# Half of the score masks and the experts' weights on ScalarE, longer DRAM packets and a new written order in a fused S4 convolution and mixture-of-experts kernel

## The chip, the cores and the metric

The kernel runs on one core of a Trainium2 chip. The metric is device time in microseconds (us). Before the change the median of three runs is 816.15 us (811.91 to 817.66); a fourth execution was taken with the hardware profiler.

The core's engines run side by side, each through its own list of instructions in order: TensorE (PE in the profile; its weight loads are PEld), VectorE (DVE), ScalarE (ACT), GpSimd (POOL) and SyncE (SP). SP issues most DMA transfers, and POOL issues the indirect gathers and the accumulating stores. 16 DMA engines carry all of them.

## The reference, cut to what matters

```python
x = A_u                       # [1, 2048, 448]
xn = _layernorm(x)
return x + _A_ref(xn, ...) + _B_ref(xn, ...)

def _A_ref(u, A_re, A_im, B_re, B_im, C_re, C_im, log_dt, Dskip):
    P = jnp.exp(logdA[:, :, None] * l[None, None, :])     # [448, 256, 2048], complex
    K = jnp.einsum("dn,dnl,dn->dl", Cc, P, dB).real
    ...                       # y = causal convolution of u with K over L = 2048, by FFT
    return y + u * Dskip

def _B_ref(x, w_q, k1, k2, u, v):     # 16 heads, 64 + 64 keys, 4096 experts, K = 1
    q = jnp.einsum("nd,dhc->nhc", xf, w_q)
    s1 = jnp.einsum("nhd,ed->nhe", q[..., :dk], k1)
    s2 = jnp.einsum("nhd,ed->nhe", q[..., dk:], k2)
    ...                       # best key of each half gives the expert, e = i1 * 64 + i2
    act = _gelu(jnp.einsum("nd,nhkd->nhk", xf, u[top_e]))
    out = jnp.einsum("nhk,nhk,nhkd->nd", g, act, v[top_e])
    return out
```

## The kernel before, in words

**Work.** The 2048 tokens are 16 tiles of 128; the 448 channels are four chunks (128, 128, 128, 64).

- *Weights.* `combine` loads the query weights of each of 16 heads (`wq`, L855, two loads of 448 KB a head) and multiplies them by the keys, so a score is one product with a token tile. `params` loads the six S4 parameter arrays (L419) and prepares exponents and phases.
- *Score stage, 16 tiles.* `ln` normalizes a tile. `score` forms 32 rows of 64 scores a token: TensorE writes four quarters `sc` of 128x512 into PSUM (L961, L970). They and other products share the tag `s2`, which has three buffers. VectorE takes each row's maximum (`mx`, L985). A mask of the places that are not the maximum follows: for quarters 0, 1 and 2 VectorE does it in one `not_equal` (L992), for quarter 3 ScalarE does eight `Sign` activations of 128x64 (L996). The option `SG` is the number of quarters that ScalarE takes. A quarter's buffer is free when its mask is done. From the masks VectorE finds the expert numbers, which go through DRAM to become gather indices.
- *S4 kernel, 56 batches of eight channels.* `batch` and `products` build powers of the state matrix: phases on VectorE (L614), sines and absolute values on ScalarE (L629 to L635), exponentials on ScalarE (L590, L592), products on VectorE (L660 to L666), then small matmuls (L682, L702).
- *Convolution.* `conv` does a transform for each chunk. Its result `tq` goes to the DRAM scratch `t_d` (L842), 512 bytes a packet in the three wide chunks.
- *Experts, 16 tiles of four groups.* For each group of four heads four indirect gathers bring 128 rows of 896 floats (`ue`, L1083). VectorE multiplies the first half by the token and sums it (`dot`, L1091). Then, on 128x4 values: a square on ScalarE (L1098), a product on VectorE (L1101), the gate's product on VectorE (L1110), tanh on ScalarE (L1104), a product on VectorE (L1107). VectorE spreads the four weights over a 0/1 mask into `A`, 128x128 (L1114), and TensorE adds the weighted second halves into `po` (L1121). When the four groups are in, ScalarE copies `po` out (L1132), and POOL adds it onto the output in DRAM (L1135).
- *Final.* For each chunk `final` loads `t_d` back (`tl`, L1165), multiplies (L1177), and adds to the output; for the last chunk it loads the output so far (`bb`, L1155), adds on VectorE (L1181) and stores (L1189).

**What sets the order.** Each stage adds steps to a plan: a stream name, an engine, a cost in ns, the instructions, and the buffers that it takes and gives. The order is written out by hand as a string, `ORDER` (L173 to L202): each character names a stream (its place in `CODE`), and each occurrence issues that stream's next step. The string has 3421 steps. Each engine works through its steps in this order, and a step that is not ready holds up what is behind it on its engine. Buffers of the tag `q` (22 of 128x1024) hold gathers, score weights, transform inputs and loads alike; a gather can start when an earlier holder has been released.

Of the kernel before, what the change touches and what calls it, by code (L numbers as in the profile page):

```python
# [32 lines left out]
def shape_consts():  # L33
# [17 lines left out]
    pe = 2 * np.pi * (np.outer(k2, b) % 64) / 64  # L51
# [64 lines left out]
class Plan:  # L116
# [57 lines left out]
    "41H444446H4447H244024HHHH424HH6H4H2H7H12H4HHHHHII7H42H1HNCC42H7282O42D2E842HH8748HH121CDH4CD2KHF4HEE1D14E224HFL4H4CKL7DC"  # L174
    "I472K24F72EC4I4F3MD7777E7Y3C5QFJLKL9D56DCEFEP47F48D47C9F9EM8KQLQ48D9FwK97774E7FC4L8K44DCJA947E449YC87C9JFDD47E46H7RF4798"
    "AL8QRCEARF7ADCZDEDRFEFEFKQRHwQLNORHGQ9RHQQPH9SaRRMRTQZHTRQYQNATRRHTRHHJOATSTQQTTTTBRTeHReTTGQTUVQGHbYVMHHWRRQQHHXHxxcHee"
    "RRRPdfSNgxgOyfeHgHHwgQwQIHHIyxPfQKyHgygzggxRQJ!gRT!gHhRYTQLTGRzHgQhTKh#xgHRLxTfRMRNOPeSQygyJxXgx#TQ$yTxgeHQHTfQTyTThxTzR"
    "!HgRg!bHxTfgxRgzTQRe#Q#yyyUycgdz$NybxxRO!Qch!ezRyVQHhH#Rdebyi#STTVIIgxRRHThhYwj$gwyzh!QxK!wgyHQzWTLHRwRQKxLRQHRxy#TN#kR$"
    "HxPMhShghyxyxHOHizxaygHQXH!TyxTjTeK!QThJLTyy%kbXeRzhHRQ&RQKRiJzxP#jHf!Qg#$!eyHHLYRQzhggHkfRghieHHRxxgxSf#jK#ykTyI$lLKTgg"
    "LMeTyZlzmTKm!x!LlKyxzmLlN#xUHM#Tyx$IOgggTxgQTYQwKPhHHQyHfHQyTRwgzLwg!R!gQxhgRhRKgzMhyHTe#HfJHgHw#gLmQxHeehxx$yRyhiNRReeO"  # L180
    "yxjkfgzQQ!gVHVhSP!xg%yTyHzJxTyTHx#QRT#gHxTTyQglRHzThchQ$gH!hTIMdKgg!YQR&TIxRRLWmyYKLiNJhjhzfyR#OgUJk#R$ihaQHjexPyVyHxHeH"
    "zKSkMxgegy!x!hHQfTLHRKzyTexLgMR#g#eVQhfH$HbRgQgwQwglhyWxwZTxXygghyHwHzlRggRmHmH!Yg!TRzyTxiQf#xjke#RHy$HSNOHHIyhxTxlTz!TT"
    "TXXK!yTghQLTzQ#yeTPegxhKhgJhx%#fgmeyxgyIQxyezyLifg$Hjg!cQbRkRhKTg!YgLRzxlKh#UQHg#MgVgx$dQygaRLxHiNyhHxHmzOfPQeygw!R!xjhy"
    "ggzkefgyRRSgxyQ&##RHwQRThhzRVw!HHH$fxTQl!zH##QRehHQgRgiyRHHxgeWRSxewNMHjHxO$HhkTIyhgQgZKLyTxQhlJyTxmyTgKLRigmTQzhx!T!zIx"
    "#xygyMfJ%xgJXTQyPeRRTRg#hx$TgTjfzekQKgy!TRgx!Lxfyhz#y#lTegQRxKUgc$LmeNRSVxVeayOhWhzywQ!hTQiQyRjxgy!hQzygwhRPhXzgxgMT#Rxk"
# [12 lines left out]
    "ezhgfwyjgwey-gex#yg#xeiyzgxyg!kal$yj!zx%yxhyxghmkz#hc!#hg$ydglxeghfyymggixfgheyegfe!jzh#k#xezg!ylg!Zxgzxhggyy#iggh$yhz#$"
    "wwg!jhkmlymxfwoheyxexh!giphgwqego&oypfxepqqyz#ohx#yxggoz!ppfqg!yjy$gxzeoyr#gqxxozphngigqkoxpgs#%aq!yxo!z$yhpg#ghqejsfpno"
    "gehyrggphs&hyxe#tzfgq$kegofgnxygi!qg!jhexzphxouxqpo#gvnk#ghyqywwpxgwhg$qsihgojyfyezg!kx!pzqopehetgrghhsshoyny#whfuglxlx#"  # L200
    "qmpgymiefvjhgzx$egxgykulx!gmlg!x%yqytxnihymzglgghxhxghr&shhhzixjs#j#k!lvh$mmy!kizxt##jlkyl(ymum$vooqoqyzqy!x!rs)yq,qsqry"
    "(*zsosrsq#xy(zsq)!+!r)*sts+t#t$t*(z#.#+$%.)/:&.-//.::/*;+;;:;")  # L202


class Kernel:
    OPT = dict(UE=8, XX=4, CS=2, ZI=2, MG=4, KT=4, HL=2, SG=1, XR=4, OB=3, XT=1, ST=1)
# [21 lines left out]
    def alloc(s):  # L228
# [11 lines left out]
        s.t_d = dr.tile([64, 2, 32, D], F32, name="t_d")  # L240
# [146 lines left out]
    def params(s, part):  # L387
# [349 lines left out]
    def conv(s, ck, VK):  # L737
        p = s.p
# [31 lines left out]
        for q in range(4):  # L770
# [76 lines left out]
    def combine(s, h):  # L847
# [219 lines left out]
    def experts(s, t):  # L1067
# [9 lines left out]
        for g in range(4):  # L1077
            Q = {}
            u = (4 * t + g) / 64
            for c in range(4):  # L1080
# [25 lines left out]
            def v2(Q=Q):  # L1106
                s.nc.vector.scalar_tensor_tensor(Q["th"], Q["th"], 1.0, Q["dot"], op0=ALU.add, op1=ALU.mult)  # L1107

            def v2b(g=g, Q=Q):
                s.nc.vector.tensor_tensor(out=Q["dot"], in0=Q["dot"], in1=s.IDX[t][:, :, 4 + g].bitcast(F32), op=ALU.mult)  # L1110

            def v2c(Q=Q):
                Q["A"] = s.sm.tile([128, 4, 32], F32, name="A", bufs=2)
                s.nc.vector.tensor_tensor(out=Q["A"], in0=s.mask[:, None, :].to_broadcast([128, 4, 32]),  # L1114
                                          in1=Q["th"][:, :, None].to_broadcast([128, 4, 32]), op=ALU.mult)
# [23 lines left out]
    def final(s, ck):  # L1139
# [20 lines left out]
        for g in range(4):  # L1160
            B = {}

            def l1(B=B, g=g):
                B["tl"] = s.flat("q", "tl", 8 * w).rearrange("p (x d) -> p x d", x=8)
                s.nc.sync.dma_start(B["tl"], s.t_d.rearrange("(x c) r k d -> x (c r k) d", c=2)[8 * g:8 * g + 8, :, d0:d0 + w].rearrange("x p d -> p x d"))  # L1165
# [95 lines left out]
```

## Time and profile before

| | |
|---|---|
| Median of three runs | 816.15 us (811.91 to 817.66) |
| Profiled execution | 807.42 us, its span 805.7 us |
| Mean granted TensorE clock | 0.906 |
| Gathers (L1083) on POOL | 256, 308.2 us |
| Score matmuls (L961) | 384, 181.2 us |
| Experts' dots (L1091) | 256, 155.7 us |
| Changes of ScalarE's table in the exponentials and the sines (L590, L639) | 54 loads of 1.283 us |

The page names an instruction by engine, line, operation and tiles, `out<-in`. A group's row gives its count, busy time in us and mean ns of one behind the bar, and then the engine's idle time just before the group with what ended it. Where instructions of a group overlap, busy time is less than count times mean. A row of a stretch gives from:to, its length, the busy time of each engine (and how many instructions), the granted TensorE clock, the busy share of the 16 DMA engines and GB/s. A wait's row gives us in total, times, and the longest. The chain of waits is the work that ended last, followed back from the end.

### The profile page before, as it was taken

The page shows a single profiled execution, that of the slowest core. Times are in us where ns is not written, and L with a number is a line of the kernel's source. Part 1 is how long each engine was busy: PE and PEld are TensorE (multiplying, and loading weights), DVE is VectorE, ACT ScalarE, POOL GpSimd, SP SyncE. Part 2 cuts the span into 40 slices and gives each one's busy share as a digit, 9 for nine tenths or more (in the row PEclk, how much of TensorE's full clock was granted, in tenths as well). Part 3 has the DMA queues.
Part 4 walks back from the last instruction along what each step waited for, and adds up shares of the span by engine and source line. Part 5 has one row for each costly group of instructions (what it writes and reads, how often), then busy time and mean ns, then how long its engine had stood idle before and what let it go on. Part 6 is the DMA issues. An engine that isn't in the chain of part 4 may idle for free.

```text
span 805.7 us, 19880 instructions
## 1 busy us (share of the span) xinstructions
PE 664.6 (82%) x7628; PEld 361.1 (45%) x7628; DVE 686.9 (85%) x1727; ACT 533.3 (66%) x1069; POOL 351.6 (44%) x303
## 2 busy tenths in 40 slices
PE   1999999989999899799887877778885865899693
PEld 0433333343443334344364644445663532567472
DVE  6885678998899989799998989899998888999850
ACT  1665246538576676564567868888788887888630
POOL 2020033234333435347745474765364557643521
PEclk9999999999999999999999995678997665699896
DMA  9997666778867668588999998999699999889899
GB/s 313 348 335 263 259 224 175 232 204 249 275 199 242 202 202 255 180 252 270 366 300 312 304 286 286 292 291 276 206 286 344 319 222 269 252 264 287 271 253 175
DMA packets 139975, 212.36 MB, mean 264 GB/s; under 512 B 45096, under 2 KB 121896, under 8 KB 139816
## 3 DMA queue, kind: packets, MB, share of 16 engines
q0 software_dynamic: 29120, 124.27, 49.9%
q1 hardware_dynamic: 110760, 86.81, 35.5%
q8 instruction: 60, 0.98, 0.5%
q14 instruction: 35, 0.29, 0.1%
HBM read 181.42 MB, written 33.29 MB: 267 GB/s over the span
## 4 chain that ended last, share of the span: by engine, by line
DVE 33%; PE 24%; ACT 15%; DMA 15%; issue 9%; POOL 2%; SPq 1%; POOLq 0%; DVEq 0%; ACTq 0%
PE sc L961 8%; DVE ue L1091 7%; DMA ue<-in_uv_dram,ig 6%; DVE ph L614 4%; PE wc L862 3%; DVE mg L666 3%; PE po L1121 3%; DVE zi L662 2%; DVE cp L808 2%; ACT CS L635 2%; DVE mx L985 2%; ACT CS L629 2%; ACT CS L632 2%; PE sc L970 2%; PE up L724 2%
## 5 line engine op out<-in xcount | busy, mean ns | idle before, releaser
L1083 POOL DMA_INDIRECT ue<-in_uv_dram,ig x256 | 308.2, 1204 | 364.2 <-PE po L1121 101.4
L961 PE MATMUL sc<-W,xt 128*128 128x512 f32 x384 | 181.2, 611 | 8.6 <-ACT xt L946 7.8
L1091 DVE SCALAR_TENSOR_TENSOR ue<-ue,xr 128x448 f32<-128x448 f32 x256 | 155.7, 619 | 26.0 <-DMA ue<-in_uv_dram,ig 24.1
L961 PEld LDWEIGHTS sc<-W,xt 128*128 128x128 f32 x384 | 69.3, 191 | 100.8 <-issue 86.2
L1121 PE MATMUL po<-ue,A 128*32 128x448 f32 x512 | 74.0, 654 | 23.4 <-DVE A L1114 9.2
L682 PE MATMUL kp<-mg 128*32 128x64 f32 x1792 | 65.8, 244 | 22.2 <-DVE mg L666 7.9
L590 ACT ACTIVATE mg<-lg 128x512 f32<-128x512 f32 x112 | 63.1, 603 | 17.2 <-PE lg L579 16.7
L682 PEld LDWEIGHTS kp<-mg 128*32 128x32 f32 x1792 | 48.1, 124 | 49.4 <-issue 13.2
L662 DVE TENSOR_TENSOR zi<-mg,CS 128x1024 f32<-128x1024 f32 x56 | 68.3, 1219 | 0.0
L666 DVE TENSOR_TENSOR mg<-mg,CS 128x1024 f32<-128x1024 f32 x56 | 68.3, 1219 | 0.0
L682 PE MATMUL kp<-zi 128*32 128x64 f32 x1792 | 65.7, 242 | 0.0
L614 DVE CUSTOM_DVE_ANT_0 ph<-st,ph 128x512 uint16<-128x512 uint16 (+2 forms) x84 | 65.2, 776 | 0.5
L635 ACT ACTIVATE CS<-CS,halfpi 128x1024 f32<-128x1024 f32 x56 | 64.4, 1150 | 0.8
L629 ACT ACTIVATE CS<-ph 128x1024 f32<-128x1024 int32 x56 | 62.0, 1107 | 3.9 <-DVE ph L614 3.1
L632 ACT ACTIVATE CS<-ph 128x1024 f32<-128x1024 int32 x56 | 62.6, 1117 | 0.0
L702 PE MATMUL vp<-f,kt 128*64 128x128 f32 x448 | 41.3, 317 | 19.5 <-DVE kt L693 11.3
L985 DVE TENSOR_REDUCE mx<-sc 128x8 f32<-128x512 f32 x64 | 43.7, 683 | 14.5 <-PE sc L970 9.6
L682 PEld LDWEIGHTS kp<-zi 128*32 128x32 f32 x1792 | 50.3, 126 | 0.2
L579 PE MATMUL lg<-lc,rt 32*128 32x512 f32 x112 | 38.8, 544 | 12.0 <-ACT mg L590 7.9
L830 PE MATMUL ip<-cp,e 64*128 64x256 f32 x384 | 44.7, 382 | 2.9 <-DVE cp L808 2.8
L702 PEld LDWEIGHTS vp<-f,kt 128*64 128x64 f32 x448 | 27.5, 155 | 43.1 <-DVE kt L693 16.7
L798 PE MATMUL U<-VU,g 128*64 128x128 f32 x384 | 41.3, 294 | 6.0 <-ACT us L803 3.4
(244 smaller groups left out, 1219.2 us busy)
## 6 DMA issues: line engine op xcount, KB each, us to landing
wq<-in_wq_dram SPq DMA_DIRECT2D x32, 448.0 KB
xr<-xn_d SPq DMA_DIRECT2D x64, 224.0 KB
vu_d<-vst SPq DMA_DIRECT2D x64, 112.0 KB
VU<-vu_d SPq DMA_DIRECT2D x12, 512.0 KB
t_d<-tq SPq DMA_DIRECT2D x24, 256.0 KB
tl<-t_d SPq DMA_DIRECT2D x12, 512.0 KB
ue<-in_uv_dram,ig POOLq DMA_INDIRECT x256
xx<-in_x_dram SPq DMA_DIRECT2D x16, 224.0 KB
```

Of the source, the lines that this page charges most:

```text
L614: s.nc.vector.tensor_tensor(out=rw(n, 2 * n), in0=rw(0, n), in1=o["st"][:, k, b0:b0 + 2].rearrange("p b h m x -> p (b h m x)")[:, None].to ...
L629: s.nc.scalar.activation(CS[:, 1].rearrange("p (m r x) -> p m r x", r=16, x=2), four(s.ph), AF.Sin, scale=SC)
L632: s.nc.scalar.activation(B["CS"][:, 0].rearrange("p (m r x) -> p m r x", r=16, x=2), four(s.ph), AF.Abs)
L635: s.nc.scalar.activation(B["CS"][:, 0], B["CS"][:, 0], AF.Sin, scale=-SC, bias=s.halfpi)
L662: V.tensor_tensor(out=zi[:, 512:], in0=mg[:, 512:], in1=CS[:, 1], op=ALU.mult)
L666: V.tensor_tensor(out=mg[:, 512:], in0=mg[:, 512:], in1=CS[:, 0], op=ALU.mult)
L682: s.nc.tensor.matmul(kp[32 * c:32 * c + 32, 64 * gi:64 * gi + 64], T[ri][:, 1024 + m:1056 + m], view(T[ri], m, [[512, 2], [1, 32]]), start ...
L702: s.nc.tensor.matmul(vp[64 * ri:64 * ri + 64, 128 * gi:128 * gi + 128], B["kt"][:, 64 * gi:64 * gi + 64], s.f1[:, ri], start=True, stop=True)
L961: s.nc.tensor.matmul(B["sc", q].rearrange("p a b -> p (a b)"), B["xt"][:, i], w, start=(q % 2 == 0 and i == 0), stop=(q % 2 == 1 and i == 2))
L1083: s.nc.gpsimd.indirect_dma_start(out=ue, out_offset=None, in_=s.io["uv"], in_offset=bass.IndirectOffsetOnAxis(ap=s.IDX[t][:, c, g:g + 1].b ...
L1091: s.nc.vector.scalar_tensor_tensor(Q["ue", c][:, :D], Q["ue", c][:, :D], 1.0, B["xr", c], op0=ALU.mult, op1=ALU.mult, accum_out=Q["dot"][: ...
L1121: s.nc.tensor.matmul(B["po"][32 * c:32 * c + 32, :D], Q["A"][:, c], Q["ue", c][:, D:], start=(g == 0), stop=(g == 3))
```

## The change

- `SG` goes from 1 to 2: quarter 2's mask is also made by eight `Sign` activations on ScalarE.
- The four experts' weights of a group are spread by four ScalarE copies of 128x32, each with a per-partition scale (a new stream `e_A`), in place of VectorE's one product of 128x128.
- The product of the dots with the gate is written to a tile of its own, `dw`, instead of over `dot`. It depends on the dots alone, and the tanh no longer waits for it.
- Layouts in DRAM: `wq` and the six parameter arrays are stored so that one partition's row is one run of 3584 bytes instead of two of 1792. `t_d` becomes one array a chunk, with the two parities of the block number apart; the transform's constant `e` is permuted to match. The store keeps packets of one channel row (512 bytes in the wide chunks). The load reads eight such rows in one run (4096 bytes), with two transfers of 64 partitions in place of one of 128.
- A new `ORDER`, again of 3421 steps. Near the end all four loads of the last chunk stand ahead of the last load of the output so far.

```diff
-    pe = 2 * np.pi * (np.outer(k2, b) % 64) / 64
+    pe = 2 * np.pi * (np.outer(k2, b.reshape(32, 2).T.reshape(64)) % 64) / 64
...
 ORDER = (
-    "41H444446H4447H244024HHHH424HH6H4H2H7H12H4HHHHHII7H42H1HNCC42H7282O42D2E842HH8748HH121CDH4CD2KHF4HEE1D14E224HFL4H4CKL7DC"
...
+    "444441442H4142444424HH7HH2H1HH227HHHH444HHH2HHHH26IN2HH444I4H6CH74H701CHD4HD18E2HH4HC28E8DO4H47CFCK28DD72HH2ILFEC44EECFK"
...
-    OPT = dict(UE=8, XX=4, CS=2, ZI=2, MG=4, KT=4, HL=2, SG=1, XR=4, OB=3, XT=1, ST=1)
+    OPT = dict(UE=8, XX=4, CS=2, ZI=2, MG=4, KT=4, HL=2, SG=2, XR=4, OB=3, XT=1, ST=1)
...
-        s.t_d = dr.tile([64, 2, 32, D], F32, name="t_d")
+        s.t_d = [dr.tile([2, 32, 2, 32, w], F32, name="t_d%d" % i) for i, (d0, w) in enumerate(s.chunks)]
...
-                s.nc.sync.dma_start(B[n], io[n].rearrange("(t p) d -> p t d", p=128))
+                s.nc.sync.dma_start(B[n], io[n])
...
-                    s.nc.sync.dma_start(s.t_d[:, ri, 8 * q:8 * q + 8, d0:d0 + w],
+                    s.nc.sync.dma_start(s.t_d[ck][ri, 8 * q:8 * q + 8].rearrange("k c x d -> (c x) k d"),
                                         Q["tq"][64 * ri:64 * ri + 64].rearrange("p k h d -> p (k h) d"))
...
-                s.nc.sync.dma_start(B["w", sd], s.io["wq"][h, sd].rearrange("t p d -> p t d"))
+                s.nc.sync.dma_start(B["w", sd], s.io["wq"][h, sd])
...
-                        for k in ("dot", "x2", "th"):
+                        for k in ("dot", "x2", "th", "dw"):
...
             def v2(Q=Q):
-                s.nc.vector.scalar_tensor_tensor(Q["th"], Q["th"], 1.0, Q["dot"], op0=ALU.add, op1=ALU.mult)
+                s.nc.vector.scalar_tensor_tensor(Q["th"], Q["th"], 1.0, Q["dw"], op0=ALU.add, op1=ALU.mult)
 
             def v2b(g=g, Q=Q):
-                s.nc.vector.tensor_tensor(out=Q["dot"], in0=Q["dot"], in1=s.IDX[t][:, :, 4 + g].bitcast(F32), op=ALU.mult)
+                s.nc.vector.tensor_tensor(out=Q["dw"], in0=Q["dot"], in1=s.IDX[t][:, :, 4 + g].bitcast(F32), op=ALU.mult)
 
             def v2c(Q=Q):
                 Q["A"] = s.sm.tile([128, 4, 32], F32, name="A", bufs=2)
-                s.nc.vector.tensor_tensor(out=Q["A"], in0=s.mask[:, None, :].to_broadcast([128, 4, 32]),
-                                          in1=Q["th"][:, :, None].to_broadcast([128, 4, 32]), op=ALU.mult)
+                for c in range(4):
+                    s.nc.scalar.activation(Q["A"][:, c], s.mask, AF.Copy, scale=Q["th"][:, c:c + 1])
...
-            y = p.chain("e_v1", "DVE", [(75, v1), (75, v2b)], deps=[y])
+            y = p.add("e_v1", "DVE", 75, v1, deps=[y])
+            yw = p.add("e_v1", "DVE", 75, v2b, deps=[v])
             y = p.add("e_a", "ACT", 100, a2, deps=[y], tset="E|S|A")
-            y = p.chain("e_v2", "DVE", [(75, v2), (dv(128), v2c)], deps=[y, s.C["mask"]], take=("A",), give=("gel",))
+            y = p.add("e_v2", "DVE", 75, v2, deps=[y, yw])
+            y = p.add("e_A", "ACT", 460, v2c, deps=[y, s.C["mask"]], take=("A",), give=("gel",))
...
-                s.nc.sync.dma_start(B["tl"], s.t_d.rearrange("(x c) r k d -> x (c r k) d", c=2)[8 * g:8 * g + 8, :, d0:d0 + w].rearrange("x p d -> p x d"))
+                for c in range(2):
+                    s.nc.sync.dma_start(B["tl"][64 * c:64 * c + 64], s.t_d[ck].rearrange("r k c x d -> c (r k) x d")[c, :, 8 * g:8 * g + 8])
...
-        wq=np.ascontiguousarray(f("B_w_q").reshape(D, 16, 2, 2, 128).transpose(1, 2, 3, 4, 0)),
+        wq=np.ascontiguousarray(f("B_w_q").reshape(D, 16, 2, 2, 128).transpose(1, 2, 4, 3, 0)),
...
-        **{n: tr("A_" + n) for n in ("A_re", "A_im", "B_re", "B_im", "C_re", "C_im")},
+        **{n: np.ascontiguousarray(tr("A_" + n).reshape(2, 128, D).transpose(1, 0, 2)) for n in ("A_re", "A_im", "B_re", "B_im", "C_re", "C_im")},
```

More of the change, by code (lines that the diff above doesn't have):

```diff
@@ L178 @@
[L178 to L185, printed above, removed]
@@ new lines @@
+    "#HHHTTxxyIy$QR%gRQfTxeNTxhhyyxhThyzIO!yg!ISizzJ!!z#Mhjg$#TRwhYZU$HSKJYwHQTeQgHTR%HLQHRKQ%LggcHRwHJVxdQxwygycHHQxNHRxOihT"
+    "yhQHTTxHhRHVRHHahgSyMQSKzLkT!z&gPQihTKy!HjgIxxTx#yTTj$TRdykQIyzfWR%LRgRhQxThRQgfKS!khPiLzgXxljY!HeRMTe#$gmxSlkfxxKyyy%Lg"
+    "Y(yKHgmLMTKLzxlH!JUNeO!Gz#Hgx$QmeyexgHyhggQ%gKLyRQhbgfhHyQhRxQgxwMzxwgRRHgHHHT!!ze#Pfxhgg$QlfKRTyee%RVHwLygHyHTN&hwOyHSz"
+    "QHT!HxmITeh!hzSe#QiRQxjg$kVRxgIMgZXyxTyyyhz!zYg!gPa#Tc%x$lhKQJRTQyL%xxYgdgmHHxHeRhygyiTKQRTHRjTThLTNWxOxfSSkeHQgijHygKTe"
@@ new lines @@
+    "hyyJTUzLMVeQfKhg(xQgVL!f!ezxRyH#QyghgM$hwbXgxz%ixPgR!kbQlzR!XgwwgThHRJHRYQlgmWxTgejR#khySHx$%yfNHSywThgHyHHeHOzQgHh!TIKL"
+    "xexxzmK!g&QLyIeT#hlfxgZygHimyMyz$T!Y%Rzxf!xK#TgThRTgHjhkTegQx$LHhHcKQdRHTghTPgTyUgiQ%gjHHyXxQLgNfRhayHyRgheezHOS!HgPzxQg"
+    "lRm!HhHV#fQyQHSggxHxyykxHxyfz!hHR$wIMTRVRRwQ%QgQgNTTRghlhe!TRzOx#yexxyeiQSITwyS$wK%JQyjzggghTkhilRh!QRmgxjxTzgPTTh!mT&#L"
+    "KfQg$gTLgxexxT%JfQyeeRZb(xTKQyyyzgLKTUgRye!!zyR#fexLyM$gxyhRahNzO%xgghywxQikySgQQ!lwJVgxzScxy!yjR#$%RVRkxgzQhh!gziQQxdNj"
@@ new lines @@
+    "yhTwTgTTRleRxSm!TJXwmR#ekyxO$xxhShZyhP%&xyyxQfggbzMgyTyP!Wxe!QxRQTlTeTfzyQTR#Tgg$zfTRx%QgiTy!yxyQxxjhRyT!eRzzgn!h#h!$%yR"
+    "yhkUnnXNgOzgQilVhSx#yxS$%ymgz!QgmjgQ!QThfRwgWzgwnwxwygTxRkhygf#$ReVe%xQgRxgfeeyPlyxzgQmgg&hx!coexx!aRhyyRzSySyxzh!Tp!#Tx"
+    "gxzT$xyqx%nhxox#oyyiT(pyxz$!TxyTTq!hyTXz%wgdjpky#nbxo(xqxnwpoyghigpgzqe$gfgqohgWrpfT!wgTgheo!hfhqTssxogeepzoxyqTig%pUVqt"
+    "#epgXyhjwy.$hgrgZnx%yhokjg&sqhggypyikoezx!yqyhoz!xx(xfgpge#$zVyyqg!%fyxspoe!qhegzgxfgop#pgxxyhqoh$qpzjxyek!hcoglygztygrx"
@@ new lines @@
+    "!yhd#z!Xmw%qhglpm$xisjlmsqibjwzgyhk!krfx#gwaxwxglhWg%xh$gmlmslf%yggfgetheyiehehgygmexyh&zhgjsgixhkh!y!yxlgxmfyxxxgzjgzh!"
+    "gzekl!hm#$h%ihgehyg#x(xxyyy$fxxyzgg!ehejtf!gieyyggzZgkhyh#lg%g)*jzmghg+hZigck$wajxhd!ykfw%gle!eze)gh#$fhxgegwyh%fg&wyygg"
+    "egz!xzhi*h+jglxgmx)ky!#m$gxxflxyy%h,xh)ygzhmyh!e!egggyij(xxzefx#gykeey$ynwhgywxh*f+%gggz!!gglgzx(ia#hhgmj*hkgelyweywbXh+"
+    "gehzXm$fgigfjggfgxy,xghe!xchh%x,ek!zglgxgdxg#mi$xhh%y,hjgkyxlmxonyhygzgifepgyoxgxhoq!hfyzpq&oyjp!qoe#pz!!z$obx#$gxnqyepg"
```

32 lines of the change are left out of this document (12 added, 20 removed).

## The prediction

> **What bounds the kernel now.** I read the page's first line, engine shares and chain first, then the DMA queues, then the stretches, because the kernel has stages with different limits. I cut it at 60 us (weights loaded), 405 us (last score tile's signs done) and 750 us (tail).
>
> ```profile
> span 805.7 us, 19880 instructions
> PE 664.6 (82%) x7628; PEld 361.1 (45%) x7628; DVE 686.9 (85%) x1727; ACT 533.3 (66%) x1069; POOL 351.6 (44%) x303
> DVE 33%; PE 24%; ACT 15%; DMA 15%; issue 9%; POOL 2%; SPq 1%; POOLq 0%; DVEq 0%; ACTq 0%
> q0 software_dynamic: 29120, 124.27, 49.9%
> q1 hardware_dynamic: 110760, 86.81, 35.5%
> ```
>
> No engine is full: VectorE, TensorE and the DMA engines each work over 80% of the span, and the chain changes hands.
>
> ```profile
> core 0: us, PE busy (x) PEld busy (x) DVE busy (x) ACT busy (x) POOL busy (x), PEclk, DMA share, GB/s
> 0.00:60.00 60.00, 40.85 (x167) 16.92 (x169) 47.12 (x79) 29.93 (x65) 9.42 (x19) 1.00 0.97 331
> 60.00:405.00 345.00, 317.63 (x2195) 135.12 (x2193) 301.42 (x802) 202.38 (x455) 133.09 (x117) 0.99 0.76 239
> 405.00:750.00 345.00, 269.22 (x4504) 181.09 (x4500) 315.09 (x786) 283.66 (x511) 193.75 (x155) 0.82 0.93 281
> 750.00:806.00 56.00, 36.91 (x768) 27.95 (x768) 23.29 (x63) 17.28 (x40) 15.30 (x15) 0.80 0.94 230
> ```
>
> Three things to see. The first 60 us are loads (DMA share 0.97). From 60 to 405 us TensorE is fullest: 317.6 of 345 us (92%), idle 27.4, with VectorE at 301.4 (87%) and ScalarE at only 202.4 (59%). From 405 to 750 us VectorE leads with 315.1 of 345 (91.3%), and ScalarE is no longer a spare engine: 283.7 (82%).
>
> **The change part by part.**
>
> ```profile
> L992 DVE TENSOR_TENSOR eq<-sc,mx 128x512 bf16<-128x512 f32 x48 | 32.9, 686 | 2.9 <-DMA vu_d<-vst 2.6
> L996 ACT ACTIVATE eq<-sc,mx 128x64 bf16<-128x64 f32 x128 | 27.9, 333 | 14.5 <-DVE mx L985 14.4
> L996 ACT ACTIVATE eq<-sc,mx x128: 306/332/376, 81.0 to 403.3; 128x64 bf16<-128x64 f32 x128
> L1114 DVE TENSOR_TENSOR A<-mask,th 128x128 f32<-128x128 f32 x64 | 18.3, 286 | 0.5
> L1110 DVE TENSOR_TENSOR dot<-dot,ig 128x4 f32<-128x4 f32 x64 | 10.2, 160 | 0.4
> ```
>
> *Masks.* Each of 16 tiles has four score quarters; one more goes from VectorE to ScalarE. VectorE loses 16 x 0.686 = 11.0 us. ScalarE gains 16 blocks of eight signs, 27.9/16 = 1.74 us each: 27.9 us. The signs run from 81.0 to 403.3 us (smallest, median and largest are 306, 332 and 376 ns), so all of this lies before 405 us.
>
> *Experts' weights.* 64 VectorE products of 0.286 us go (18.3 us); 256 ScalarE copies of 128x32 with a per-partition scale come. No row shows that copy. The nearest is the sign of 128x64, which also reads a per-partition operand: one alone takes 333 ns, but eight together 1.74 us, so the next begins (1740-333)/7 = 201 ns after the last. A column costs about 0.83 ns (128x512 against 128x126 out of PSUM, rows below: (603-276)/386 = 0.85). With 32 columns fewer I estimate 306 ns alone, 175 ns between starts, a group of four 3 x 175 + 306 = 0.83 us, 64 of them 53 us. Ends: 0.57 us (four copies 90 ns apart, as the 128x4 square below, which starts at 530.36 and is followed at 530.45, plus one of 306 ns) and 1.22 us (four that don't overlap). I take 0.83, since the sign is the nearest.
>
> ```profile
> L590 ACT ACTIVATE mg<-lg 128x512 f32<-128x512 f32 x112 | 63.1, 603 | 17.2 <-PE lg L579 16.7
> L690 ACT ACTIVATE kt<-kp 128x126 f32<-128x126 f32 x56 | 15.4, 276 | 13.6 <-PE kp L682 13.4
> 530.36 0.21 ACT L1098 ACTIVATE x<-dot 128x4 f32<-128x4 f32 x1
> 530.45 1.10 ACT L632 ACTIVATE CS<-ph 128x1024 f32<-128x1024 int32 x1
> ```
>
> [...]
>
> How they fall on the stages:
>
> ```profile
> 60.00:405.00 345.00, 7.11 (x25) 0.99 0.76 239
> 405.00:750.00 345.00, 10.02 (x35) 0.82 0.93 281
> 750.00:806.00 56.00, 1.16 (x4) 0.80 0.94 230
> ```
>
> (L1114's VectorE time alone.) To 405 us VectorE loses 11.0 + 7.1 = 18.1 us, ScalarE gains 27.9 + 25 x 0.83 = 48.7, to 251 of 345 (73%). From 405 to 750 VectorE falls to 305.1, ScalarE rises by 35 x 0.83 = 29.0 to 312.7 (90.6%): the two change places.
>
> *Dots in a tile of their own.* The L1110 product leaves the path between the two ScalarE steps: 0.16 us a group shorter. The weights' copies make the path 0.83 - 0.29 = 0.54 longer and put a second trip to ScalarE into it, where they queue behind exponentials and sines. Behind them wait the po matmuls, whatever TensorE has after those, and the gathers, whose buffers these matmuls free:
>
> ```profile
> PEld po L1121 <- DVE A L1114: 16.6, 19, 2.0
> POOL ue L1083 <- PE po L1121: 101.4, 31, 8.5
> ```
>
> So +0.38 us a group, 24 us over 64 groups if nothing covered it. The cover is distance in the written order: I counted steps from a group's first gather to its po matmul, median 115 of 3421 before and 106.5 after; last weight to matmul, 10 and 10. The new order makes the round shorter, so I cost the latency at nothing; without that cover it is up to the 24 us.
>
> *Long packets.* wq and the six parameter loads go from 256 to 128 packets each, tl from 1024 to 128: 38 x 128 + 16 x 896 = 19,200 packets fewer of 139,975, same bytes. q1's packets average 784 B and 16 x 0.355 x 805.7/110760 = 41 ns, q0's 4268 B and 221 ns: 53 and 52 ns per KB, so a fixed cost per packet does not show (saving 0). The other end, 41 ns for any packet spared, is 19,200 x 41/16 = 49 us of DMA time, 7 us at DMA's 15% of the chain. I take 2.5: 1 in the loads, 1.5 from 405 us on. tl becomes two transfers, 16 more issues on SP; one took 0.44 us (row below, under the written order), 7 us, spread over SP's waits and 1.8 us in the tail.
>
> [...]
>
> *Written order.* Exp and sine still alternate: 60 changes of table set counted in either order. The four residual copies (input to output, in DRAM) move from steps 275 to 420 to steps 286 to 743, further into the stretch where the DMA share is 0.76; I cost that at nothing, with the idle quarter of the DMA engines as the cover. In the tail SP waits for the last output and only then issues the last tl load:
>
> ```profile
> 787.25 6.86 DMA out_dram<-ob
> 794.12 0.67 SPq L1155
> 794.91 0.44 SPq L1165 DMA_DIRECT2D tl<-t_d  x1
> 794.91 3.88 DMA tl<-t_d
> 798.93 1.11 PE po L1177 x32
> 800.07 0.42 DVE bb L1181
> ```
>
> The new order issues all four tl loads ahead of that wait, so 3.88 us leave; the last base load (issued at 794.12, its first use at the earliest some 2 us later) is late next. I take -2.5, of which the extra issues give 1 back: -1.5.
>
> *Sum.* Loads -1. To 405 us: between 18.1 x 33% (VectorE's share of the chain) = 6.0 and all 18.1; TensorE is fullest and I take -8. From 405 to 750: the fullest engine was 91.3% busy; ScalarE's 312.7 at that share is 342.5 us (-2.5), VectorE's 305.1 would be 334 (-11); I take the later, -2.5, and -1.5 for packets. Tail -1.5. Total -14.5 from this execution's 807.4 (span 805.7 and 1.7 around it): 792.9. The median of the runs shown, 816.15, lies 8.7 above this execution, so 801.6.
>
> **The rivals.**
>
> *VectorE was the only bound (faster still).* All -18.1, -11, -1, -1.5, -1.5: -33.1, 783 on the median's scale. Against it: TensorE has only 27.4 us idle to 405 us, and ScalarE is at 90% later.
>
> *ScalarE takes the place (no change).* If the four copies do not overlap (1.22 us), ScalarE has 283.7 + 35 x 1.22 = 326.4 us, at 91.3% full 357.5: +12.5 where I have -2.5. Total +0.5: 816.6. For it: the rows above at 82% already.
>
> *PSUM banks are held too long (slower).* A score bank is free after its mask, 0.69 us on VectorE, now 1.74 us on ScalarE plus its queue there; three banks serve four quarters of a tile, and TensorE, with 27.4 us of slack, waits in order.
>
> ```profile
> ACT eq L996 <- DVE mx L985: 14.4, 7, 4.0
> ```
>
> That row says the sign mostly waits for nothing but its turn. If the turn comes behind a sine block's half (1.7 us), 16 x (1.05 + 1.7) = 44 us of later release; half of it on TensorE is 22, and the -8 is gone: 807.4 - 1 + 22 - 4 - 1.5 = 822.9, 831.6 on the median's scale. It eats the whole gain from 14.5 us of lost TensorE time on.
>
> *The granted clock falls (slower).* Rows of the same kernel at two clocks:
>
> ```profile
> 600.00:650.00 50.00, 34.66 (x592) 20.30 (x588) 44.02 (x106) 43.71 (x76) 28.34 (x24) 0.76 1.05 317
> 650.00:700.00 50.00, 35.04 (x510) 19.25 (x512) 44.05 (x115) 40.86 (x71) 31.13 (x25) 0.56 0.88 256
> 745.57 0.96 PE L1121 MATMUL po<-ue,A 128*32 128x448 f32 x8
> 762.64 1.72 PE L1121 MATMUL po<-ue,A 128*32 128x448 f32 x8
> ```
>
> If waits for ScalarE bring 405 to 750 us to the 0.66 of these two stretches, TensorE's 269.2 us become 269.2 x 0.82/0.66 = 334, 366 at 91.3% full: +21 for my -2.5. Total +9, 825. [...]
>
> **How the numbers follow.** My sum 0.44; VectorE alone 0.09; ScalarE in its place 0.19; banks 0.15; clock 0.13. A measurement tells about 1% (8 us) from no change. My case holds 790 to 812 around 801.6; a fifth of it, 0.08, is above 808, as its 14.5 us gain is the size of the latency I cost at nothing. Faster: 0.36 + 0.09 = 0.45, and 0.05 of ScalarE's case where VectorE gains more early: 0.50. Same: 0.08 + 0.14 = 0.22. Slower (above 824.3): 0.28. The range goes from 786, leaving out most of VectorE alone (0.07), to 830, leaving out half the slower cases (0.12).
>
> **What would show it.** Right: VectorE near 658 us, ScalarE near 614; the weights' line at 0.83 us a group; TensorE over 92% busy to 405 us; ScalarE fullest after; no tl load behind the last base load. Wrong: copies near 1.2 us a group; TensorE waiting for signs; a clock below 0.75 after 405 us; gathers waiting for po matmuls well over 101 us.

## The result and the profile after

The changed kernel takes 820.65 us (median of 20 runs, 816.17 to 825.20) against 814.65 us of the kernel before beside it (20 runs): a ratio of 1.0127 with a 95% interval of [1.0096, 1.0158]. That ratio is taken over each kernel's runs within 1.5% of its fastest, which leaves out 7 of the 20 runs before, and so is larger than the ratio of the two medians, 1.0074. The change is slower by 6 to 10 us, where the prediction said 1.8% faster. The profiled execution took 818.54 us. Its page begins, in the order of the lines shown of before (span, engines, chain, q1):

```profile
span 815.5 us, 20337 instructions
PE 679.4 (83%) x7628; PEld 376.5 (46%) x7628; DVE 663.4 (81%) x1647; ACT 609.2 (75%) x1453; POOL 344.6 (42%) x303
PE 38%; ACT 22%; DMA 17%; DVE 13%; issue 5%; POOL 1%; SPq 1%; ACTq 0%; DVEq 0%; POOLq 0%
q1 hardware_dynamic: 91816, 86.82, 35.2%
```

The engines were relieved and loaded nearly as planned: VectorE lost 23.5 us (686.9 to 663.4; 29.3 were planned), ScalarE gained 75.9 (533.3 to 609.2; 80.9 were planned). In the chain VectorE fell from 33% to 13%, but TensorE rose from 24% to 38% and ScalarE from 15% to 22%. On q1 19,000 packets are gone, and their time is what it was: 0.352 x 815.5 = 287 us of 16 engines, 0.355 x 805.7 = 286 before.

The stretches, cut as before, show TensorE at 320.9 of 345 us (93%) up to 405 us, VectorE down to 291.2 there, and ScalarE level with VectorE after 405:

```profile
0.00:60.00 60.00, 39.96 (x175) 16.47 (x177) 40.74 (x72) 29.12 (x64) 8.54 (x18) 1.00 0.91 321
60.00:405.00 345.00, 320.87 (x2131) 138.42 (x2125) 291.21 (x762) 249.30 (x679) 129.41 (x114) 0.99 0.75 241
405.00:750.00 345.00, 269.35 (x4320) 183.64 (x4320) 296.76 (x727) 298.33 (x630) 182.62 (x152) 0.80 0.92 273
750.00:816.00 66.00, 49.24 (x1008) 37.94 (x1006) 34.64 (x88) 32.50 (x84) 23.98 (x19) 0.92 0.97 240
```

How far the work had come is read from the first and last start of one line. Of the score matmuls, before first and after second:

```profile
L961 PE MATMUL sc<-W,xt x384: 592/592/1057, 40.2 to 400.6; 128*128 128x512 f32 x192
```

```profile
L961 PE MATMUL sc<-W,xt x384: 592/592/1222, 38.7 to 400.3; 128*128 128x512 f32 x192
```

The last score matmul starts at 400.3 us where it started at 400.6. So between these two traces nothing was gained in the stage where 8 us were expected, and the 9.8 us of the span were lost behind it. (One trace of each is a thin base for the first half of that: in a second trace of the changed kernel, n_again below, the last score matmul starts at 395.5 us, and its span is 816.8 us all the same.) Two things in the trace could be the reason. First, TensorE waits for the weights that ScalarE now makes (rows: waiter, line, releaser, us in total, times, longest). For the kernel before these waits are

```profile
PE po L1121 <- DVE A L1114: 9.2, 12, 1.7
```

on PE and 16.6 us on PEld (row shown in the prediction). After:

```profile
POOL ue L1083 <- PE po L1121: 136.5, 37, 16.3
PEld po L1121 <- ACT A L1115: 32.9, 30, 5.4
PE po L1121 <- ACT A L1115: 22.4, 15, 5.2
```

Second, VectorE waits for the token rows `xr` of the experts' dots, for which it hardly waited before. Rows of before and after:

```profile
DVE ue L1091 <- DMA xr<-xn_d: 0.9, 1, 0.9
```

```profile
DVE ue L1091 <- DMA xr<-xn_d: 16.1, 8, 5.6
```

The worst of it is in the first chunk's final loads. The timeline (start, us, instruction; in brackets the idle time before it and its end) of SP, VectorE, ScalarE and TensorE there:

```profile
493.09 1.12 SPq L1168 DMA_DIRECT2D tl<-t_d  x2
494.25 0.58 SPq L1171 DMA_DIRECT2D hl<-in_h_dram  x1
494.94 1.68 SPq L1075 DMA_DIRECT2D xr<-xn_d  x2
```

```profile
512.76 0.63 DVE L1091 SCALAR_TENSOR_TENSOR ue<-ue,xr 128x448 f32<-128x448 f32 x1 [5.60 <-DMA xr<-xn_d]
...
515.68 0.63 DVE L1091 SCALAR_TENSOR_TENSOR ue<-ue,xr 128x448 f32<-128x448 f32 x1 [2.29 <-DMA xr<-xn_d]
...
516.23 1.22 DVE L614 CUSTOM_DVE_ANT_0 ph<-st,ph 128x2048 uint16<-128x2048 uint16 x1
```

```profile
517.48 1.06 ACT L629 ACTIVATE CS<-ph 128x1024 f32<-128x1024 int32 x1 [7.69 <-DVE ph L614]
...
519.12 0.60 ACT L1187 ACTIVATE tl<-po 128x512 f32<-128x512 f32 x1
...
519.76 1.12 PE L702 MATMUL vp<-f,kt 128*64 128x128 f32 x8 [10.25 <-ACT tl L1187]
```

Read it from the bottom: TensorE is idle for 10.25 us, until ScalarE has emptied a product's buffer; ScalarE has stood 7.69 us before its sines, for the phases; VectorE could not make the phases, because in its order two dots stand before them, and these waited 5.60 and 2.29 us for `xr`. SP had issued `xr` rows by 496.6 us, right behind two halves of a `tl` load on the same queue. (The chain of waits gives this stretch to a `tl` load of 13.12 us. The brackets show otherwise; where one wait has several semaphores, the chain takes the one that ended last by its reckoning.) The stretch shows how late `xr` rows can reach TensorE; it does not show what they cost, for in the second trace of the changed kernel the same wait of TensorE is 1.20 us. Both leads go on to the experiments: ScalarE's copies, and the DMA queue behind the `tl` loads.

The end of the chain shows the tail as ordered: the `tl` loads no longer stand behind the last base load, but each takes two transfers, and the last landing at 808.13 us is again what the end waits for:

```profile
796.22 3.26 DMA t_d<-tq
...
803.05 5.08 DMA tl<-t_d
808.13 0.04 issue
808.17 1.79 PE po L1180 x62
```

### The profile page after: what moved, and what is told of

Its sections match the earlier page's. It is cut to its first block, busy times and chain, and to the rows that moved or that the text cites. A ratio compares the mean times of both kernels' runs of the same rounds, so it can differ in the third digit from the quotient of the medians.

```text
span 815.5 us, 20337 instructions
## 1 busy us (share of the span) xinstructions
PE 679.4 (83%) x7628; PEld 376.5 (46%) x7628; DVE 663.4 (81%) x1647; ACT 609.2 (75%) x1453; POOL 344.6 (42%) x303
## 4 chain that ended last, share of the span: by engine, by line
PE 38%; ACT 22%; DMA 17%; DVE 13%; issue 5%; POOL 1%; SPq 1%; ACTq 0%; DVEq 0%; POOLq 0%
PE sc L961 13%; DMA ue<-in_uv_dram,ig 6%; DMA xr<-xn_d 5%; PE po L1121 4%; DVE ue L1091 4%; PE sc L970 3%; PE kp L682 3%; ACT CS L632 3%; ACT CS L635 2%; ACT CS L629 2%; DMA tl<-t_d 2%; PE U L798 2%; PE wc L862 2%; PE ip L830 2%; ACT A L1115 2%
## 5 line engine op out<-in xcount | busy, mean ns | idle before, releaser
L1083 POOL DMA_INDIRECT ue<-in_uv_dram,ig x256 | 300.3, 1173 | 379.8 <-PE po L1121 136.5
L1121 PE MATMUL po<-ue,A 128*32 128x448 f32 x512 | 86.2, 633 | 22.5 <-ACT A L1115 22.4
L702 PE MATMUL vp<-f,kt 128*64 128x128 f32 x448 | 43.4, 325 | 28.3 <-DVE kt L693 11.7
L1115 ACT ACTIVATE A<-mask,th 128x32 f32<-128x32 f32 x256 | 61.3, 324 | 3.3 <-DVE th L1107 3.3
L996 ACT ACTIVATE eq<-sc,mx 128x64 bf16<-128x64 f32 x256 | 55.6, 348 | 10.7 <-DVE mx L985 10.7
L830 PE MATMUL ip<-cp,e 64*128 64x256 f32 x384 | 47.2, 393 | 2.3 <-DVE cp L808 2.2
```

Of the source, the lines that this page charges most:

```text
L702: s.nc.tensor.matmul(vp[64 * ri:64 * ri + 64, 128 * gi:128 * gi + 128], B["kt"][:, 64 * gi:64 * gi + 64], s.f1[:, ri], start=True, stop=True)
L1083: s.nc.gpsimd.indirect_dma_start(out=ue, out_offset=None, in_=s.io["uv"], in_offset=bass.IndirectOffsetOnAxis(ap=s.IDX[t][:, c, g:g + 1].b ...
L1115: s.nc.scalar.activation(Q["A"][:, c], s.mask, AF.Copy, scale=Q["th"][:, c:c + 1])
L1121: s.nc.tensor.matmul(B["po"][32 * c:32 * c + 32, :D], Q["A"][:, c], Q["ue", c][:, D:], start=(g == 0), stop=(g == 3))
```

## The experiments

Theories. *Hand-over*: moving work to ScalarE lengthens the path to `po` and costs what VectorE's relief gains. *Order*: the new written order costs by itself. *Layout*: one of the DRAM layouts costs. Every ratio below is to the kernel before on the same chip. The runs fell on five chips; on two of them everything, the kernel before included, is slower (medians of before 857 and 860 us, on the other three 812 to 814), and these two are named where they appear.

### The parts of the change

**o_all**: all edits of the change in the written order of before (the copies stand in the old place of the product, quarter 2's signs in the old place of its mask).

```diff
-ORDER = (new)
+ORDER = (old)
-p.add("e_A", "ACT", 460, v2c, ...)
+p.add("e_v2", "ACT", 460, v2c, ...)
```

> The changed kernel with the written order of before: signs of quarter 2 and the weights' copies on ScalarE, dots in their own tile, new layouts, each in the slot where before made them. If the new order is the cause (less work between a transfer's issue and its use), the ratio to before falls to 0.985 to 1.00 and VectorE's waits for xr fall from 16.1 us to under 3. If ScalarE's added 76 us are the cause, it stays at 1.01 or goes above, since this order was not made for them, with po waiting over 30 us for A. If the t_d layout is the cause, it stays at 1.01 with late tl loads.

Measured: 847.09 us, 1.0426 [1.0370, 1.0482]. Its waits:

```profile
PEld po L1121 <- ACT A L1115: 42.8, 31, 4.7
PE po L1121 <- ACT A L1115: 28.3, 16, 4.3
ACT A L1115 <- DVE th L1107: 18.6, 16, 2.9
```

TensorE waits 28.3 us for the copies, against 9.2 for the product before, and ScalarE itself stands 18.6 us before copies that are not ready (3.3 us in the changed kernel). VectorE's wait for `xr` falls to 4.6 us, and yet the kernel is slower. The edits alone are a loss; the new order is part of what makes them bearable.

**n_bothdve** and **n_wdve**: the new order, with masks and weights back on VectorE, and with the weights alone back.

```diff
-for c in range(4):
-    s.nc.scalar.activation(Q["A"][:, c], s.mask, AF.Copy, scale=Q["th"][:, c:c + 1])
+s.nc.vector.tensor_tensor(out=Q["A"], in0=s.mask[:, None, :].to_broadcast([128, 4, 32]),
+                          in1=Q["th"][:, :, None].to_broadcast([128, 4, 32]), op=ALU.mult)
...
-if q not in sign:
+if q < 3:                     # n_bothdve alone: quarter 2's mask on VectorE
```

> The changed kernel, new order, with quarter 2's mask and the weights' product back on VectorE in the same slots. If ScalarE's work is the cause: 0.995 to 1.00. If the new order or the layout is the cause: 1.01 to 1.03, since VectorE gets its 29 us back and the transfers stay late.

> The changed kernel, new order, with only the weights' product back on VectorE in the same slot. If the copies' 61 us on ScalarE and the longer way to po are the cause: 0.995 to 1.003, and po's wait for A falls from 22 us to about 9. If the order is the cause: 1.01 to 1.02.

Measured: 830.82 us, 1.0249 [1.0204, 1.0294], and 828.18 us, 1.0204 [1.0164, 1.0245]. Without the edits the new order is worse than with them. Order and edits belong together: neither is good for anything without the other, and so "the order costs by itself" is no full account either. The waits of n_wdve speak against *hand-over* as a full account too:

```profile
PEld po L1121 <- DVE A L1114: 21.1, 17, 3.1
PE po L1121 <- DVE A L1114: 14.6, 13, 2.4
```

Without the copies TensorE waits less for the weights (14.6 us in place of 22.4, where 9 were expected), and the kernel is slower, not faster. The gathers' wait for `po`, 101.4 us before and 136.5 after, is 133.7 us in n_bothdve: it rises with the new order even without a single copy on ScalarE.

**n_oldlay**, and on a second chip **n_oldlay2**: the changed kernel with all old DRAM layouts. **n_oldtd2**: with the old layout of `t_d` alone.

```diff
-s.t_d = [dr.tile([2, 32, 2, 32, w], F32, name="t_d%d" % i) for i, (d0, w) in enumerate(s.chunks)]
+s.t_d = dr.tile([64, 2, 32, D], F32, name="t_d")
...
-for c in range(2):
-    s.nc.sync.dma_start(B["tl"][64 * c:64 * c + 64], ...)
+s.nc.sync.dma_start(B["tl"], ...)
...
```

> The changed kernel, new order, with all three DRAM layouts of before (t_d, wq, parameters). If the layout of t_d (4 KB runs 32 KB apart) makes its transfers late: 0.99 to 1.00, and tl no longer in the chain. If the order or ScalarE is the cause: 1.008 to 1.02, within 0.5% of the changed kernel.

> The changed kernel with all old DRAM layouts, again, on one chip with the changed kernel. If the layouts cost 1.5%, it is 0.010 to 0.020 below the changed kernel's ratio. If what the first two comparisons showed was the difference of two chips, the two lie within 0.005.

> The changed kernel with the old t_d alone, again. If t_d is what costs, it stands with all old layouts; if wq and the parameters do, with the changed kernel; if neither does by itself, all three lie within 0.005.

> The changed kernel itself once more, so that it stands on the same chip as the two below: 1.008 to 1.016 by every theory.

Measured: n_oldlay 813.71 us, 0.9974 [0.9933, 1.0016]. On the second chip n_again, the changed kernel unaltered, 818.66 us, 1.0113 [1.0075, 1.0151]; n_oldlay2 810.78 us, 0.9994 [0.9957, 1.0030]; n_oldtd2 811.44 us, 0.9983 [0.9935, 1.0031]. The loss is the layout of `t_d`, and all of it: with the old `t_d` the kernel is as fast as before. `wq` and the parameters make no difference. In the profile of n_oldtd2 the waits for the copies are still there:

```profile
PEld po L1121 <- ACT A L1115: 30.8, 31, 5.4
PE po L1121 <- ACT A L1115: 18.5, 13, 5.2
```

So with these waits in place VectorE's relief and the new order together are worth 0 to -2 us of 812, inside the interval. That it is the hand-over that takes the gain is not shown: n_wdve, without it, was slower.

**o_lay**: the counter-test, the old order with masks and weights on VectorE, and of the change only the new layouts and the dots' own tile.

> The kernel before, old order, masks and weights on VectorE, with the new DRAM layouts and the dots' own tile alone. If the layouts themselves cost: 1.010 to 1.020. If they do nothing: 0.995 to 1.005.

Measured: 821.11 us, 1.0108 [1.0041, 1.0176]. The layouts cost the same 1.1% in the order of before. (Over this kernel, o_all prices ScalarE's edits in the old order: 1.0426/1.0108 = 1.031, with both intervals some 1.023 to 1.040, 25 us. n_bothdve prices the new order without the edits: 1.0249/1.0108 = 1.014, some 1.006 to 1.022, 11 us. n_again has both, and stands at 1.0113/1.0108 = 1.000. o_all and n_bothdve ran on another chip than the other two. So order and edits each lose alone, and together they come out level.)

### What of the layout costs

The layout changes three things of the load: its transfers (two of 64 partitions for one of 128), its packets (4096 bytes for 512), and the distance between rows in DRAM. A first set of runs fell on a slow chip:

> The changed kernel with only t_d, its store and its load as before (wq and the parameters stay long). If t_d's new layout costs the 1.5%: 0.990 to 1.003, as with all three old layouts. If wq and the parameters cost it: 1.010 to 1.015.

> The changed kernel with only wq and the parameter arrays as before (two runs of 1792 bytes); t_d stays new. If t_d costs the 1.5%: 1.010 to 1.016. If wq and the parameters do: 0.990 to 1.003.

> The changed kernel with 4 KB of padding after each row of the new t_d, so that rows stand 36 KB apart instead of 32 KB (20 instead of 16 KB in the last chunk); same packets, same two loads. If the power-of-two distance is what costs: 0.990 to 1.003, and the 4096-byte packets fall from a mean of 233 ns to about 190. If the packet's length or the split of the load is: 1.010 to 1.016.

> The changed kernel with t_d as before (512-byte packets), but each load still split in two transfers of 64 partitions. If the split (16 more transfers on SP, each on half the partitions) costs: 1.008 to 1.016. If the place of the data in DRAM or the packet's length does: as the unsplit old t_d, 0.990 to 1.003.

Measured there, against 860.1 us before: n_oldtd 1.0112 [1.0057, 1.0167], n_oldwp 1.0078 [1.0036, 1.0120], n_padtd 1.0078 [1.0024, 1.0133], n_half 1.0113 [1.0075, 1.0151]. All four alike: inconclusive. Even n_oldtd, level with the kernel before on other chips, loses 1% on this one (0.4% between the medians of all runs, 863.7 and 860.1 us), so the time there is set by something else. The set was repeated on a chip of the usual speed:

- **n_oldtd3**, the old `t_d`, as the reference.
- **n_half2**: the old `t_d` with its 512-byte packets, the load in two halves of 64 partitions.
- **n_padtd2**: the new `t_d`, each row of DRAM 4 KB longer.
- **n_cfirst**: a `t_d` with the half outermost, so that one transfer of 128 partitions reads 4096-byte packets; the store becomes four transfers of 32 partitions in place of two of 64.

```diff
-s.t_d = [dr.tile([2, 32, 2, 32, w], F32, ...) ...]
+s.t_d = [dr.tile([2, 2, 32, 32, w], F32, ...) ...]
...
-for c in range(2):
-    s.nc.sync.dma_start(B["tl"][64 * c:64 * c + 64], s.t_d[ck].rearrange("r k c x d -> c (r k) x d")[c, :, 8 * g:8 * g + 8])
+s.nc.sync.dma_start(B["tl"], s.t_d[ck].rearrange("c r k x d -> (c r k) x d")[:, 8 * g:8 * g + 8])
```

> The changed kernel with the old t_d layout and its one load of 128 partitions, as the reference for this chip. On two chips it stood at 0.998 of the kernel before, on a slower third chip at 1.011. Expected by all theories: 0.998, within 0.005.

> The old t_d layout (512-byte packets), but its load issued in two halves of 64 partitions as the changed kernel does. If it is the second transfer of each load that costs (16 more issues on SyncE's queue, two landings to wait for): 1.011 of the kernel before. If it is the DRAM layout (4 KB packets, or 32 KB between rows): 0.998, no different from the kernel with one load.

> The new t_d layout, each row of DRAM lengthened by 4 KB, so that rows are 36 KB apart and not 32 KB; packets and transfers as in the changed kernel. If rows at a power of two meet in the same part of the memory: back to 0.998 of the kernel before. If the packets' length or the second transfer costs: 1.012, no different from the changed kernel.

> A t_d layout with the half (c) outermost: the load is one transfer of 128 partitions with 4 KB packets, and the store is four transfers of 32 partitions a group in place of two of 64. If the load's second transfer costs: back to 0.998 of the kernel before, or up to 1.003 with the stores' 24 more issues, each of which lies earlier and has slack. If the 4 KB packets cost: 1.011.

| kernel | transfers x partitions | packet | median us | ratio to before |
|---|---|---|---|---|
| n_oldtd3 | 1 x 128 | 512 B | 809.88 | 0.9988 [0.9951, 1.0024] |
| n_half2 | 2 x 64 | 512 B | 824.27 | 1.0135 [1.0078, 1.0193] |
| n_padtd2 | 2 x 64 | 4096 B | 820.29 | 1.0114 [1.0061, 1.0167] |
| n_cfirst | 1 x 128 | 4096 B | 808.31 | 0.9964 [0.9936, 0.9993] |

The table reads down one column: two transfers of 64 partitions cost 1.1 to 1.35%, with short packets and with long ones, and padding does not help. Against the one-transfer kernel with the same packets it is 1.0135/0.9988 = 1.015 and 1.0114/0.9964 = 1.015, and n_again over n_oldtd2 was 1.013: 10.5 to 12 us. One transfer costs nothing, and with long packets in one transfer the kernel is the fastest of this set, if only by 0.4%. The layout is not what costs; the load in halves is. (n_half2 and n_oldtd3 differ in nothing else; n_cfirst also has its store in four transfers.) The loss comes late: the last score matmul starts at 395.5 us in n_again and 397.1 in n_oldtd2, at 398.7 in n_padtd2 and 401.3 in n_cfirst, so the whole of it lies behind, where the `tl` loads are.

Why the halves are dear shows on q1. Rows of two kernels of the same chip, span and q1 (packets, MB, share of 16 engines), n_cfirst and n_padtd2:

```profile
span 807.8 us, 20342 instructions
q1 hardware_dynamic: 92072, 86.82, 34.7%
```

```profile
span 818.6 us, 20337 instructions
q1 hardware_dynamic: 91816, 86.82, 35.6%
```

Same bytes, packets equal to 0.3%, and 0.356 x 818.6 = 291.4 us of DMA time in place of 0.347 x 807.8 = 280.3: the packets of the halves are slower. The same with short packets on the slow chip, n_oldtd and n_half:

```profile
span 857.9 us, 20301 instructions
q1 hardware_dynamic: 105896, 86.81, 33.6%
```

```profile
span 871.3 us, 20337 instructions
q1 hardware_dynamic: 106152, 86.82, 34.9%
```

288.3 and 304.1 us. Packet by packet the trace has, for the 4096-byte loads from 470 to 530 us, a median of 159 ns in n_cfirst, and with halves 278 in n_padtd2 on the same chip, 268 in n_again and 229 in the changed kernel's first trace.

**n_xsplit** tells apart whether that comes from there being two transfers or from each writing half the partitions: n_cfirst with its load in two transfers again, cut along the rows x, so that each writes all 128 partitions. **n_cfirst2** beside it is n_cfirst again.

```diff
-s.nc.sync.dma_start(B["tl"], ...[:, 8 * g:8 * g + 8])
+for c in range(2):
+    s.nc.sync.dma_start(B["tl"][:, 4 * c:4 * c + 4], ...[:, 8 * g + 4 * c:8 * g + 4 * c + 4])
```

> The layout of n_cfirst, its load again in two transfers, but cut along the eight rows x that each partition takes: each transfer writes all 128 partitions, with 2 KB packets. Number of transfers, semaphores and bytes as in the changed kernel. In the changed kernel a 4 KB packet of these loads took 268 ns (median, 470 to 530 us), in n_cfirst 159 ns. If writing only 64 partitions is what slows the packets and costs the 1.1 to 1.35%: 2 KB packets near 80 ns, and 0.997 of the kernel before, as n_cfirst. If two issues and two landings cost: 1.011.

> n_cfirst again, beside n_xsplit on one chip. It stood at 0.9964 [0.9936, 0.9993] of the kernel before; expected 0.994 to 0.999. If it is under 1 again it is the best version of the study, by less than half a per cent.

These two fell on the second slow chip (before: 857.48 us): n_xsplit 864.13 us, 1.0092 [1.0051, 1.0133], and n_cfirst2 868.53 us, 1.0110 [1.0038, 1.0181]. They don't differ in time, which on such a chip says little, as the first set shows; that n_cfirst is better than the kernel before was not confirmed. Their DMA rows say more, n_cfirst2 and n_xsplit:

```profile
span 863.3 us, 20342 instructions
q1 hardware_dynamic: 92072, 86.82, 33.0%
```

```profile
span 860.3 us, 20365 instructions
q1 hardware_dynamic: 94376, 86.82, 32.9%
```

284.9 and 283.0 us: two transfers of all partitions cost the DMA engines nothing, and the trace's 2048-byte packets of n_xsplit take 84 ns in the median, 168 for two, against 159 for one of 4096 bytes. The slow chip does not hide it: n_padtd, with halves, has 265 ns on the other one. So the slow packets are due to the half set of partitions; that is shown (229 to 278 ns against 159). Why a packet into half the partitions takes longer, no run shows.

How slow packets become lost time is less clear. One path is VectorE's wait for `xr`, the loads that follow the `tl` loads on SP's queue (`DVE ue <- DMA xr<-xn_d`):

| kernel | load | chip | wait for `xr`, us |
|---|---|---|---|
| changed kernel | halves | not recorded | 16.1 |
| n_again | halves | A | 12.4 |
| n_oldlay2 | whole | A | 11.0 |
| n_oldtd2 | whole | A | 10.3 |
| n_padtd2 | halves | B | 15.5 |
| n_cfirst | whole | B | 8.9 |
| n_bothdve | halves | C | 8.7 |
| n_wdve | halves | C | 12.0 |

On one and the same chip the halves have the longer wait, by 1.4 to 6.6 us. But most of the rise from 0.9 us before is there with whole loads too, so it is not the halves', and o_lay, with halves in the old order, loses 1.1% with 6.3 us of this wait. So the wait for `xr` is at most a part of the 10.5 to 12 us; what the rest waits for was not found. On the slow chips the wait is 1.9 us in n_cfirst2 and less in n_oldtd, n_half and n_xsplit, and there n_half is level with n_oldtd, which fits, but those chips are not understood (last section).

Nor is it settled how much of the 10.5 to 12 us is the slow packets and how much the second issue of each load, since no run on a chip of the usual speed has two transfers of all partitions. Rows of the `tl` issues before and after (count, smallest, median and largest ns) come to 16 x 0.378 = 6 us of SP's time before and 32 x 0.582 = 19 after:

```profile
L1165 SPq DMA_DIRECT2D tl<-t_d x16: 359/378/4399, 489.4 to 794.9; - x16
```

```profile
L1168 SPq DMA_DIRECT2D tl<-t_d x32: 444/582/1634, 485.7 to 804.2; - x32
```

## Why the prediction was wrong

- **Loads, -1.** Nothing that can be measured: the old `wq` and parameter layouts (n_oldlay2 against n_oldtd2) are level with the new.
- **To 405 us, -8.** Failed between the two kernels. The last score matmul moved by 0.3 us. VectorE's relief was there, and TensorE was already the fullest engine, as the prediction itself said; -8 then needs 8 of TensorE's 27.4 us of idle time to be waits that end with VectorE's relief. TensorE is idle 24.1 us after the change, and 5.4 of that are waits for the copies (3.8 for the product before). The relief is not worthless, though: in the same new order without the edits (n_bothdve) the last score matmul starts at 408.3 us, and in six traces with both edits at 395.5 to 401.3 (on n_bothdve's own chip n_oldlay has 397.9).
- **Latency and written order costed at nothing.** Failed: the new order without the edits loses 1.4%, and in it the edits win back about as much (1.0249 to 1.0113), so that relief, latency and order together come out at 0 to -2 us. The prediction put a shorter round in the written order (115 to 106.5 steps) as the cover, though its own row (16.6 us on PEld for `A`) said that the cover was incomplete. The waits for `A` rose to 32.9 us on PEld and from 9.2 to 22.4 on PE; the gathers' wait for `po` rose from 101.4 to 136.5, the sign of being wrong that the prediction had named. The median distance says nothing about the groups at its low end. How much of the gain these waits take stays open: n_bothdve has 133.7 us of the gathers' wait without any copy, and n_wdve, without the copies, is slower. The other bound given, up to 24 us without cover, is near the 25 us that ScalarE's two edits cost in the old order, but that is chance, as the 25 us hold the signs too.
- **From 405 us, -2.5.** The mechanism was right: ScalarE and VectorE change places (298.3 and 296.8 us of 345). The gain did not come. TensorE's waits for the copies, 17.0 us of the 22.4, lie mostly in this stretch, and so does the whole cost of the `tl` loads.
- **Weights' copies, 0.83 us a group.** Mis-sized, with a small effect:

```profile
L1115 ACT ACTIVATE A<-mask,th 128x32 f32<-128x32 f32 x256 | 61.3, 324 | 3.3 <-DVE th L1107 3.3
L996 ACT ACTIVATE eq<-sc,mx 128x64 bf16<-128x64 f32 x256 | 55.6, 348 | 10.7 <-DVE mx L985 10.7
```

  61.3/64 = 0.958 us, inside the ends of 0.57 and 1.22. Taking columns off the sign's distance between starts was the error: put at 175 ns for a copy of 32 columns, it is (958 - 324)/3 = 211, no less than the (1738 - 348)/7 = 199 of the signs of 64 columns beside them (55.6/32 = 1.738 us a block). (A column is 0.85 ns by the rows of the prediction, not 0.83; its estimate of 0.83 us a group stays the same with it.) The signs came out as put, 55.6 - 27.9 = 27.7 us for 27.9.
- **Long packets, -1.5, and `tl` in two transfers.** The wrong sign, and the step that decides the outcome. The end "a fixed cost per packet does not show (saving 0)" came out for the whole, 19,000 packets fewer and no DMA time less, but for another reason: a fixed cost does show (27 ns for 512 bytes in the kernel before, 159 and not 216 for 4096 into all partitions in n_cfirst), and the halves took back what the long packets spared (280.3 us of q1 in n_cfirst, 287 here). The step that failed is the price of the two halves: 16 more issues and 1.8 us of tail, where they cost 10.5 to 12 us. What the prediction left out is that a packet into half the partitions is itself slower, 229 to 278 ns for 159. What stands behind these loads on their queue, the `xr` rows, pays at most a part of it (1.4 to 6.6 us more wait on the same chip).
- **Tail, -1.5.** The order did what it was said to do. What the end waits for is again a `tl` load, one of eight transfers now.
- **The rivals.** "ScalarE takes the place" is nearest in its outcome for all but the layout (no change, 0.997 to 0.999), but its mechanism, copies that don't overlap (1.22 us a group), was not the one: a group took 0.958 us. The PSUM banks were no issue: in the trace after the change PE has no wait for a sign, and PEld one of 0.8 us. The granted clock after 405 us is 0.80 for 0.82 before; that waits of TensorE lower it was not shown. No rival had the transfers' halves, though the range, 786 to 830, holds the median of 820.65 us on account of the others, which is luck.

Sum by the prediction's terms: its -14.5 us were, by the kernels with the old `t_d`, -2 to 0 (0.9974 to 0.9994); the halves add 10.5 to 12. The second is shown by the experiments. Of the first it is shown that order and edits together come out level, but not which wait keeps them there.

## What to carry to other kernels

Price a DMA by the partitions it writes before its packets: 16 loads cut into partition halves cost 10.5 to 12 us here, and the same long packets in one transfer of 128 partitions cost nothing. Before relief of the second fullest engine is put into a sum, read how much of the fullest engine's idle time is put down to the second, and read the waits for a hand-over that grows longer, not the median distance in the order. An order written out by hand belongs to the assignment it was made for: judge the two together (against the old pair the edits alone are 3.1% slower, the order alone 1.4%, and both together level).

## What the runs showed of the hardware

- A 4096-byte packet of a load into 64 partitions takes 229 to 278 ns in the median from 470 to 530 us (229 in the changed kernel's first trace, 268 in n_again, 278 in n_padtd2), of a load into 128 partitions 159 ns (n_cfirst), both beside the gathers.
- Packets eight times as long (512 to 4096 bytes) into all partitions spare little: 27 ns for 512 bytes (median of the kernel before from 470 to 530 us, the stores of `t_d` among them) is 216 for eight, against 159 for one of 4096 (n_cfirst), and the whole of q1 takes 280.3 us with the long packets (n_cfirst) and 0.352 x 808.3 = 284.5 with the short ones (n_oldtd2), half a per cent of the span.
- Chips differ by more than the change: the kernel before takes 857 and 860 us on two, 812 to 814 on three. On the two slow chips TensorE is idle longer at the smallest matmuls while it waits for nothing that the profile shows (`issue`): 60.8 to 62.9 us on PEld and 34.7 to 38.5 on PE in n_oldtd, n_half, n_cfirst2 and n_xsplit, against 13.2 on PEld in the kernel before. Waits of n_cfirst on a usual chip first, of the same kernel on a slow one second:

```profile
PEld kp L682 <- issue: 12.7, 32, 1.5
```

```profile
PEld kp L682 <- issue: 62.8, 117, 2.8
PE kp L682 <- issue: 35.1, 84, 1.2
```

  There the kernels with the new order and the edits all stand at 1.008 to 1.011 of before, whatever their loads. Whether it is the order or the edits that lose there was not measured, and why this idle time is longer on these chips, and whether it is the loss, stays open.
